# Hash attention with two expert layers: the weights' conversion at other steps, the shares one operation a step, a q fetch from GpSimd

## The chip, the cores and the metric

The kernel runs on one core of a Trainium2 chip. The metric is the device time of one execution in microseconds. Of a kernel the median of several runs is compared, and one execution beside them is profiled. The engines are TensorE (PE in the profile; its weight loads are PEld), VectorE (DVE), ScalarE (ACT), GpSimd (POOL) and SyncE (SP), which only issues DMAs. Each works through its own queue in order.

## The reference

Three layers in a row, all in float32:

```
bits(x)  = (x @ proj > 0)                        6 bits a token, for q and k
s        = q k^T / 8, masked to -1e9 where the buckets of q and k differ
attn     = softmax(s) @ v                        batch 2, 8 heads, 768 tokens, head size 64
x        = attn, heads joined                    1536 x 512
g        = elu(x @ w_in) @ w_out                 512 -> 2048 -> 512 (w_in, w_out drawn as float64)
p        = probs / (sum(probs) + 1e-9)           1536 x 4, the experts' shares
out      = sum_e p[:, e] * (relu(g @ w1[e]) @ w2[e])    4 experts, 512 -> 1024 -> 512
```

## The kernel before, in words

Every product is made of float32 values split in a high and a low part, three matmuls for one. The schedule is written out by hand: the program text gives the order of each engine's queue (`manual_schedule`), and semaphores between the queues are put in from the tiles that operations read and write. A tile is taken from a pool under a tag; a tag of a pool with one buffer (`bufs=1`, as pool `l1`) gives all its tiles the same place, one after the other.

**Attention** runs over 8 pairs of heads, 12 steps a pair (`PU`), 96 steps in all (`NU`); a step is 128 queries of one head. `att_step(u)` emits, in the order of `ORDER`: the combination of a finished half (C, `emit_comb`: ACT copies two parts out of PSUM, the second into `t1`, pool `l1`, and POOL adds them), the exponential of step u+1 (E), PE's transposes of step u (T, t), the scores of step u+2 (Q, into one PSUM bank), their minimum on DVE (N), the split of the transposed weights (H, h on ACT; L, l on DVE), a preparation (M, m, d) and a third of the product with v (V). The preparations of a pair stand at fixed steps i of the pair before it: step 0 transposes the sums of the last pair and sends them through DRAM (`prep_n`: DMA `d<-rt`, then two broadcasts `rx<-d` into the tile `rx`, tag "rx" of pool `l1`), steps 1 and 2 transpose q of the next pair (ACT copies it to `xt`, POOL splits it), step 3 makes the hash bits of q and k, steps 10 and 11 transpose k of the pair after.

`loads_step` then issues SP's DMAs: the loads of v, k and q (`load_v`, `load_qk`; i = 0, 1, 2, 4) and the placement of the next pair's q, k and bits (`place`, `place_bits`; i = 2, 3, 11). At i = 3 and 6 (`FIN_AT`) it emits `emit_fin`, which on POOL multiplies half of the last pair's result by `rx` and splits it; on i = 8 and 9 POOL splits v.

After it, in pairs 1 to 7, the list `pre` is worked off: the conversion of the first three tiles of `w_in` and `w_out` from 64-bit words to float32 (`conv_w`: 2 operations on ACT, 10 on DVE, 2 on POOL; then `consumed`, which issues the next load of raw weights on SP; then `split_w`, 4 on POOL), 18 entries for one tile. `PRE_AT` lists the steps of a pair at which one entry is taken (pairs 1 to 3 for the first tile, 4 to 6 for the second); `LASTN` gives the number of entries at each step of the last pair, for the third tile. In the last pair's second half TensorE also does the first matmuls with the first tile (`l1_start(0)`, behind step 6).

The experts' shares are made of `dp`, the domain probabilities, a tile of pool `l1` under the tag "rx" too, loaded at the start: six small DVE operations into `sm` and then `pn`, which is read at 483 us. They are emitted together after step 10 (`u == PU - 2`). The first tile `rx` is allotted at step 12.

`first()` is the start: pair 0 is loaded and prepared, then SP is given the load of v, of k of pair 1, the placements of pair 0's second head, v again and the load of q of pair 1 (`load_qk(1, "q")`, L624). The tiles `sk` and `sq` have one buffer each.

Of the kernel before, what the change touches and what calls it, by code (L numbers as in the profile page):

```python
# [13 lines left out]
ALU = mybir.AluOpType  # L14
PSUM = bass.MemoryType.PSUM

P = 128
# [18 lines left out]
def lsh_attention_moe_kernel(  # L36
# [14 lines left out]
    nc = tc.nc  # L51
    B, H, S, D = q.shape
# [3 lines left out]
    E = dprobs.shape[1]  # L56
    NJ = S // P
# [48 lines left out]
    def pair(g2):  # L106

        return g2 % B, g2 // B

    def load_qk(g2, nm):  # L110
        b, hp = pair(g2)
        t = st_p.tile([P, NJ, 2, D], F32, tag="s" + nm, name="s" + nm)
        x = {"k": k, "q": q}[nm][b, 2 * hp:2 * hp + 2]
        if g2:
            nc.sync.dma_start(out=t, in_=x.rearrange("h (p j) d -> p j h d", j=NJ))
        else:
            t = t.rearrange("p j h d -> p (j h d)").rearrange("p (h j d) -> p h j d", h=2, j=NJ)
            nc.sync.dma_start(out=t, in_=x.rearrange("h (p j) d -> p h j d", j=NJ))
        raws[g2, nm] = t

    def load_v(g2, par):
        b, hp = pair(g2)
        t = st_v.tile([P, NJ, D], F32, tag="sv", name="sv")
        nc.sync.dma_start(out=t, in_=v[b, 2 * hp + par].rearrange("(p j) d -> p j d", j=NJ))
        raws[g2, par] = t
# [19 lines left out]
    dp = l1.tile([P, B * NJ, E], F32, tag="rx", name="dp")  # L145
# [7 lines left out]
    def emit_proj():  # L153
        for i in range(2):
            r, c0 = slice(i * D, (i + 1) * D), 96 + i * HB
            c = slice(c0, c0 + NB)
            hi, lo = pj[0][r, c], pj[1][r, c]
            nc.vector.tensor_copy(hi, prj[r])
            nc.vector.tensor_tensor(out=lo, in0=prj[r], in1=hi.bitcast(F32), op=ALU.subtract)
            for t in pj:  # L160
                nc.vector.tensor_scalar(out=t[r, c0 + NB:c0 + HB], in0=t[r, c].bitcast(F32), scalar1=-1.0,
                                        scalar2=None, op0=ALU.mult)
# [9 lines left out]
        x_tiles(c)  # L172
    pn = const.tile([P, B * NJ, E], F32, name="pn")

    def emit_probs():
        sm = const.tile([P, B * NJ], F32, name="psum_e")
        nc.vector.tensor_add(sm, dp[:, :, 0], dp[:, :, 1])
        for e in range(2, E):
            nc.vector.tensor_add(sm, sm, dp[:, :, e])
        nc.vector.tensor_scalar(out=sm, in0=sm, scalar1=1e-9, scalar2=None, op0=ALU.add)  # L180
        nc.vector.reciprocal(out=sm, in_=sm)
        nc.vector.tensor_tensor(out=pn, in0=dp, in1=sm.unsqueeze(2).to_broadcast([P, B * NJ, E]),
                                op=ALU.mult)

# [111 lines left out]
    def mtile():  # L298
        return (ps_m if mc[0] % 2 or mc[0] >= LASTC else ps_v).tile([P, 512], F32, tag="a", name="m")
# [6 lines left out]
    def prep_t(g2, nm, ps, j0, n):  # L306

        src = raws[g2, nm]

        def pe():  # L310
            for i in range(n):
                x = src[:, j0 + i].rearrange("p h d -> p (h d)")
                nc.tensor.transpose(ps[:, i * P:(i + 1) * P], x, ident)

        if j0 == 0:
            for part in "hl":
                stg[nm + part] = ld.tile([P, S], F32R, tag=nm + part, name=nm + part)
        cs = slice(j0 * P, (j0 + n) * P)
        hi, lo, x = stg[nm + "h"][:, cs], stg[nm + "l"][:, cs], ps[:, 0:n * P]
        sc = 1.0 if nm == "k" else -scale  # L320
        if g2:
            def act():
                xt = st_v.tile([P, HS], F32, tag="xt", name="xt")
                nc.scalar.activation(out=xt, in_=x, func=ACTF.Copy, scale=sc)
                pool_split(hi, lo, xt)

            return pe, act, None
        return (pe, lambda: nc.scalar.activation(out=hi, in_=x, func=ACTF.Copy, scale=sc),
                lambda: nc.vector.scalar_tensor_tensor(out=lo, in0=x, scalar=sc, in1=hi.bitcast(F32),
                                                       op0=ALU.mult, op1=ALU.subtract))  # L330
# [14 lines left out]
    def bits_at(g2, nm, par, half):  # L345

        r = (2 * "kq".index(nm) + half) * 32 + par * HB
        t = (ks_t if nm == "k" else qs_t)[sl(g2, par)]
        return stg["b"][r:r + HB].bitcast(F32), t[D:KM, 1, half * HS:(half + 1) * HS]

    def place_bits(g2, nm, par):
        for half in range(2):
            src, dst = bits_at(g2, nm, par, half)
            nc.sync.dma_start(out=dst.bitcast(F32), in_=src)
# [146 lines left out]
    PU = 2 * NJ  # L501
# [6 lines left out]
    EX = 0  # L508
    EU = 0
    PRE_EVERY = 3  # L510
    LASTN = (1, 2, 2, 1, 2, 1, 2, 2, 2, 1, 1, 1)
    FIN_AT = (3, 6)
    PRE_AT = (3, 4, 5, 7, 8, 9)
    MSTEP = [None] * PU
    for i, st in zip(M_AT, (("n",), ("t", "q", 0), ("t", "q", UC), ("h",), ("t", "k", 0), ("t", "k", UC))):
        MSTEP[i] = st
# [45 lines left out]
    def first():  # L562

        z = a4.tile([P, 512], BF16, tag="mk2", name="z")
        nc.gpsimd.memset(z, 0.0)
        pz = ps_v.tile([P, 512], F32, tag="a", name="pz")

        def warm(n):
            for _ in range(n):
                mm(pz, z[:, 0:P], z, start=True, stop=True)  # L570

        warm(WARM[0])
        for t in pj:
            nc.vector.memset(t.bitcast(F32), 0.0)

        for n, nm in enumerate("kq"):
            t = a4.tile([P, NJ, 2, D], F32, tag=f"mk{n}", name="s0")
            x = raws[0, nm].rearrange("p h j d -> p j h d")
            for half in range(2):
                js = slice(half * UC, (half + 1) * UC)  # L580
                if half:
                    nc.vector.tensor_copy(t[:, js], x[:, js])
                elif nm == "k":
                    nc.scalar.copy(t[:, js], x[:, js])
                else:
                    nc.gpsimd.tensor_copy(t[:, js], x[:, js])
            raws[0, nm] = t
        emit_proj()
        los = []
        for nm, pool, tags in (("k", ps_t, ("pt0", "pt1")), ("q", ps_t, ("pt2", "pt3"))):  # L590
            for half in range(2):
                ps = pool.tile([P, 512], F32, tag=tags[half], name="p" + nm)
                pe, act, dve = prep_t(0, nm, ps, half * UC, UC)
                pe()
                act()
                los.append(dve)
            if nm == "k":
                for f in los:
                    f()
                for i in range(2):  # L600
                    nc.gpsimd.tensor_scalar(out=ks_t[0][0:D, i], in0=stg["kh"][0:D].bitcast(F32), scalar1=1.0,
                                            scalar2=1.0, op0=ALU.mult, op1=ALU.mult)
                nc.sync.dma_start(out=ks_t[0][D:P, 0].bitcast(F32), in_=stg["kl"][0:D].bitcast(F32))
        for f in los[2:]:
            f()
        nc.scalar.copy(qs_t[0][0:D, 0], stg["qh"][0:D].bitcast(F32))
        nc.scalar.copy(qs_t[0][D:P, 0], stg["qh"][0:D].bitcast(F32))
        nc.vector.tensor_copy(qs_t[0][0:D, 1], stg["ql"][0:D].bitcast(F32))
        load_v(0, 0)
        load_qk(1, "k")  # L610
        warm(WARM[1])
        pe, _, dve = prep_h(mtile())
        pe()
        dve()
        for (nm, half), f in zip((("q", 0), ("k", 0), ("k", 1), ("q", 1)),
                                 (nc.scalar.copy, nc.vector.tensor_copy, nc.vector.tensor_copy, nc.scalar.copy)):
            src, dst = bits_at(0, nm, 0, half)
            f(dst, src)
        warm(WARM[2])
        for nm in "kq":  # L620
            place(0, nm, 1)
            place_bits(0, nm, 1)
        load_v(0, 1)
        load_qk(1, "q")  # L624

    first()
    for par in range(2):
        split_v(0, par)
    nc.sync.dma_start(out=dp.rearrange("p (b j) e -> p b j e", b=B),
                      in_=dprobs.rearrange("(b p j) e -> p b j e", b=B, j=NJ))  # L630
# [9 lines left out]
    def att_step(u):  # L640
# [36 lines left out]
        if g2 >= 1 and m <= NPRE and u < NU:  # L677
            if i == 0 and k_ == 0:
                pre[:] = conv_w(0, m, cv_p, 2) + [lambda: consumed(0, m, False)]
                pre.extend(lambda n=n: split_w(0, m, wpool(m), "pP", n) for n in range(2))  # L680
                pre.append(lambda: consumed(0, m, True))
            for _ in range(i in PRE_AT if m < NPRE else LASTN[i]):
                if pre:
# [489 lines left out]
        if nm in "Vk":  # L1173
            at[nm] += 1

    fin, outq = [], []
    for u in range(NU - 2):
        att_step(u)
        if u == PU - 2:
            emit_probs()  # L1180
        if u == NU - PU - 1:
            early.close()
            for i in range(2):
                raw_free.append(open_pool(f"raw{i + 2}", 1, "right"))
            open_pool("wm", 1, "right")
            loads()
        if u == NU - PU + 6:
            l1_start(0)
        take(parts, 1)
# [52 lines left out]
```

## Time and profile before

| | us |
|---|---|
| median of 3 runs (range) | 1047.69 (1045.72 to 1051.52) |
| profiled execution | 1047.5 |
| its span, first to last instruction | 1045.7 |
| PE busy | 1016.3 (97%) |
| DVE busy | 831.8 (80%) |
| ACT busy | 521.1 (50%) |
| POOL busy | 513.1 (49%) |

Attention takes the first 250 us or so, the first dense layer the time to 515, the experts the rest. Busy shares of the whole span are means over these parts. The granted clock of TensorE was 0.994 of full speed in the mean.

### The profile page before, as it was taken

How to read it: one execution, taken by the hardware profiler on the slowest of the kernel's cores; microseconds unless marked ns; L12 is line 12 of the kernel's file. 1: busy time of each engine (PE TensorE's matmuls, PEld its weight loads, DVE VectorE, ACT ScalarE, POOL GpSimd, SP SyncE). 2: the span in 40 equal slices, each digit the busy share in tenths (PEclk: the TensorE clock that was granted, in tenths of full speed). 3: DMA queues.
4: the chain of work that ended last, by engine and by line, in shares of the span. 5: the costliest groups of instructions: out<-in, count | busy, mean ns of one | idle time of the engine just before them, and what ended most of it. 6: DMA issues, size and time to landing. Idle time of an engine off the chain costs nothing.

```text
span 1045.7 us, 16064 instructions
## 1 busy us (share of the span) xinstructions
PE 1016.3 (97%) x5886; PEld 889.8 (85%) x5886; DVE 831.8 (80%) x1289; ACT 521.1 (50%) x1024; POOL 513.1 (49%) x428
## 2 busy tenths in 40 slices
PE   7999999999998999999999999999999999999996
PEld 5898999888876888888889999898898889988896
DVE  6889889988586888734557779888898888989885
ACT  5898899898564445434532333332423233233322
POOL 3466776666354345432321245545555546364554
PEclk9999999999998999999999999999999999999999
DMA  6857576561031222200020030020201102020012
GB/s 177 163 135 158 131 171 147 128 192 48 1 111 51 81 81 81 81 1 22 9 83 1 1 102 11 8 74 11 91 11 41 42 11 92 11 74 8 1 51 71
DMA packets 72694, 72.24 MB, mean 69 GB/s; under 512 B 26132, under 2 KB 60648, under 8 KB 72616
## 3 DMA queue, kind: packets, MB, share of 16 engines
q1 hardware_dynamic: 72312, 71.14, 24.7%
q8 instruction: 47, 0.77, 0.3%
q14 instruction: 31, 0.25, 0.1%
q10 hardware_dynamic: 304, 0.07, 0.0%
HBM read 48.98 MB, written 3.21 MB: 50 GB/s over the span
## 4 chain that ended last, share of the span: by engine, by line
PE 32%; issue 10%; POOL 7%; DVE 7%; ACT 1%; POOLq 0%
PE l L1018 15%; POOL a L1034 4%; PE a L967 3%; PE a L966 3%; PE a L965 3%; PE r L967 2%; PE r L966 2%; PE r L965 2%; DVE w L907 2%; DVE temps L994 1%; POOL h L750 1%; POOL hf L1000 1%; PE l L766 1%; POOL w L907 1%; DVE temps L996 1%
## 5 line engine op out<-in xcount | busy, mean ns | idle before, releaser
L1018 PEld LDWEIGHTS l<-w,op 128*128 128x128 f32 x2016 | 252.1, 188 | 13.3 <-ACT op L903 5.2
L1018 PE MATMUL l<-w,op 128*128 128x256 f32 x2016 | 255.5, 281 | 3.8 <-ACT op L903 3.8
L1034 POOL TENSOR_TENSOR a<-a,temps 128x512 f32<-128x512 f32 x84 | 124.3, 1502 | 60.0 <-DVE a L1029 60.0
L766 PE MATMUL l<-h,w 128*128 128x512 f32 x576 | 139.8, 391 | 0.1
L750 POOL TENSOR_TENSOR h<-g,h 128x512 fp32r<-128x512 f32 x44 | 66.7, 1516 | 143.2 <-ACT h L746 93.9
L766 PEld LDWEIGHTS l<-h,w 128*128 128x128 f32 x576 | 107.9, 188 | 24.5 <-POOL h L750 0.9
L1000 POOL TENSOR_TENSOR hf<-hf,temps 128x512 f32<-128x512 f32 x24 | 40.1, 1670 | 155.7 <-DVE op L907 146.9
L393 DVE TENSOR_SCALAR_CACHE_REDUCE mk<-s 128x768 f32<-128x768 f32 x96 | 91.3, 951 | 23.0 <-PE s L384 20.3
L903 ACT ACTIVATE op<-temps 128x512 fp32r<-128x512 f32 x48 | 30.1, 627 | 155.0 <-DVE temps L996 155.0
L426 DVE TENSOR_TENSOR ptl<-pt,pth 128x384 fp32r<-128x384 f32 x192 | 97.6, 550 | 11.0 <-ACT pth L429 11.0
L907 DVE TENSOR_TENSOR op<-hf,op 128x512 fp32r<-128x512 f32 x120 | 100.0, 849 | 4.4 <-ACT op L903 4.3
L903 ACT ACTIVATE op<-hf 128x512 fp32r<-128x512 f32 x120 | 74.1, 624 | 57.3 <-PE l L1018 29.9
L402 ACT ACTIVATE mk<-mk,mn 128x768 f32<-128x768 f32 x96 | 89.7, 935 | 11.5 <-DVE mk L393 10.9
L412 PE MATMUL pt<-cst,mk 128*128 128x128 f32 x576 | 94.9, 274 | 0.6 <-ACT mk L402 0.4
L383 PE MATMUL s<-ks,qs 128*128 128x512 f32 x192 | 80.2, 440 | 8.4 <-DVE mk L393 7.9
L429 ACT ACTIVATE pth<-pt 128x384 fp32r<-128x384 f32 x192 | 84.0, 482 | 8.3 <-PE pt L412 7.9
L412 PEld LDWEIGHTS pt<-cst,mk 128*128 128x128 f32 x576 | 71.0, 140 | 12.7 <-ACT mk L402 5.4
L967 PE MATMUL r<-xh,w 128*128 128x512 f32 x192 | 75.8, 395 | 0.0
L967 PE MATMUL a<-xh,w 128*128 128x512 f32 x192 | 75.6, 394 | 0.0
L966 PE MATMUL r<-xl,w 128*128 128x512 f32 x192 | 75.5, 393 | 0.0
L966 PE MATMUL a<-xl,w 128*128 128x512 f32 x192 | 75.4, 393 | 0.0
L965 PE MATMUL a<-xh,w 128*128 128x512 f32 x192 | 75.1, 391 | 0.0
(154 smaller groups left out, 2228.0 us busy)
## 6 DMA issues: line engine op xcount, KB each, us to landing
raw<-in_moe_w_dram SPq DMA_DIRECT2D x32, 512.0 KB
raw<-in_moe_w_in_dram SPq DMA_DIRECT2D x16, 512.0 KB
raw<-in_moe_w_out_dram SPq DMA_DIRECT2D x16, 512.0 KB
ks<-kh SPq DMA_DIRECT2D x15, 384.0 KB
qs<-qh SPq DMA_DIRECT2D x30, 192.0 KB
sk<-in_k_dram SPq DMA_DIRECT2D x8, 384.0 KB
sq<-in_q_dram SPq DMA_DIRECT2D x8, 384.0 KB
ks<-kl SPq DMA_DIRECT2D x16, 192.0 KB
```

The costliest lines, as they stand in the source:

```text
L393: nc.vector.tensor_scalar(out=e_t[u], in0=s_t.pop(u)[:, 0:S], scalar1=MASKED, scalar2=None, op0=ALU.min, op1=ALU.min, accum_out=mn)
L402: nc.scalar.activation(out=e, in_=e, func=ACTF.Exp, bias=mn_t.pop(u), scale=-1.0, accum_out=sums_t[g2][:, j, par:par + 1])
L412: nc.tensor.transpose(pt[:, i * P:(i + 1) * P], e_t[u][:, kb * P:(kb + 1) * P], ident)
L426: nc.vector.tensor_tensor(out=lo, in0=pt, in1=hi.bitcast(F32), op=ALU.subtract)
L766: mm(ps, a, b_, start=(m == 0 and n == 0), stop=(m == GS[g] - 1 and n == 2))
L903: nc.scalar.activation(out=hi, in_=x, func=ACTF.Copy)
L907: e.tensor_tensor(out=lo, in0=x, in1=hi.bitcast(F32), op=ALU.subtract)
L965: mm(ps, wh[:, cs], xh[c][:, ts], start=(c == 0), stop=False)
L966: mm(ps, wh[:, cs], xl[c][:, ts], start=False, stop=False)
L967: mm(ps, wl[:, cs], xh[c][:, ts], start=False, stop=(c == NC - 1))
L1018: mm(ps[:, tt * HD:(tt + 1) * HD], a[:, cs], b_[:, k_], start=(n == 0), stop=(n == 11))
L1034: nc.gpsimd.tensor_tensor(out=x, in0=x, in1=keep[nm], op=ALU.add)
```

## The change

q of pair 1 is fetched by a DMA that GpSimd issues, ahead of pair 0's hash bits, in place of the last of SP's DMAs in `first()`. The six operations of the shares are emitted one a step, behind steps 14 to 19 (from `u >= PU + 2` on). `PRE_AT` and `LASTN` are other lists, with the same sums.

```diff
-    def load_qk(g2, nm):
+    def load_qk(g2, nm, eng=nc.sync):
...
         if g2:
-            nc.sync.dma_start(out=t, in_=x.rearrange("h (p j) d -> p j h d", j=NJ))
+            eng.dma_start(out=t, in_=x.rearrange("h (p j) d -> p j h d", j=NJ))
...
-    def emit_probs():
+    def probs_steps():
         sm = const.tile([P, B * NJ], F32, name="psum_e")
-        nc.vector.tensor_add(sm, dp[:, :, 0], dp[:, :, 1])
+        yield nc.vector.tensor_add(sm, dp[:, :, 0], dp[:, :, 1])
         for e in range(2, E):
-            nc.vector.tensor_add(sm, sm, dp[:, :, e])
...
+            yield nc.vector.tensor_add(sm, sm, dp[:, :, e])
+        yield nc.vector.tensor_scalar(out=sm, in0=sm, scalar1=1e-9, scalar2=None, op0=ALU.add)
+        yield nc.vector.reciprocal(out=sm, in_=sm)
+        yield nc.vector.tensor_tensor(out=pn, in0=dp, in1=sm.unsqueeze(2).to_broadcast([P, B * NJ, E]), op=ALU.mult)
...
-    LASTN = (1, 2, 2, 1, 2, 1, 2, 2, 2, 1, 1, 1)
+    LASTN = (2, 1, 2, 0, 1, 1, 2, 2, 2, 2, 2, 1)
     FIN_AT = (3, 6)
-    PRE_AT = (3, 4, 5, 7, 8, 9)
+    PRE_AT = (3, 4, 6, 7, 9, 10)
...
         load_v(0, 0)
         load_qk(1, "k")
+        load_qk(1, "q", nc.gpsimd)
         warm(WARM[1])
...
         load_v(0, 1)
-        load_qk(1, "q")
...
-    fin, outq = [], []
+    fin, outq, probs = [], [], probs_steps()
     for u in range(NU - 2):
         att_step(u)
-        if u == PU - 2:
-            emit_probs()
+        if u >= PU + 2:
+            next(probs, None)
```

## Rows read from the trace of the kernel before

**Rows 1.** Busy time by stretch: PE, PEld, DVE, ACT, POOL, clock, DMA, GB/s

```profile
47.00:250.00 203.00, 196.34 (x1282) 178.42 (x1283) 179.03 (x375) 181.56 (x412) 131.91 (x152) 1.00 0.60 141
...
312.00:330.00 18.00, 12.98 (x46) 9.93 (x47) 12.09 (x18) 7.73 (x14) 6.91 (x4) 0.81 0.30 99
```

**Rows 2.** Timeline of PE, 0 to 60: start, us, what, [idle before <-releaser]

```profile
25.07 0.55 PE L313 MATMUL m<-cst,sq 128*128 128x128 f32 x3 [2.29 <-DMA sq<-in_q_dram]
...
47.91 0.50 PE L383 MATMUL s<-ks,qs 128*128 128x512 f32 x1 [1.20 <-DVE mk L393]
...
49.53 0.27 PE L469 MATMUL m<-cst,sums 128*12 128x128 f32 x1 [0.33 <-DVE sums L462]
```

**Rows 3.** Waits from 50 to 250: total us, times, longest

```profile
PE s L383 <- DVE mk L393: 4.6, 6, 0.9
```

**Rows 4.** Timeline of PE in the last pair

```profile
239.37 0.50 PE L383 MATMUL s<-ks,qs 128*128 128x512 f32 x1 [0.73 <-DVE mk L393]
242.37 0.50 PE L383 MATMUL s<-ks,qs 128*128 128x512 f32 x1 [0.67 <-DVE mk L393]
```

**Rows 5.** Timeline of SP's queue at the start

```profile
19.24 0.70 SPq L115 DMA_DIRECT2D sq<-in_q_dram  x1
```

**Rows 6.** Timeline of POOL at the start

```profile
7.30 1.63 POOL L601 TENSOR_SCALAR ks<-kh 64x768 fp32r<-64x768 f32 x2 [1.11 <-ACT kh L328]
11.81 0.51 POOL L135 TENSOR_SCALAR vs<-sv 128x384 fp32r<-128x384 f32 x1 [2.88 <-DMA sv<-in_v_dram]
...
21.23 0.51 POOL L135 TENSOR_SCALAR vs<-sv 128x384 fp32r<-128x384 f32 x1 [7.83 <-DMA sv<-in_v_dram]
...
29.32 1.01 POOL L136 TENSOR_TENSOR ql<-xt,qh 128x384 fp32r<-128x384 f32 x1
```

**Rows 7.** Timeline of DVE behind step 10

```profile
44.60 0.29 DVE L177 TENSOR_TENSOR psum_e<-dp 128x12 f32<-128x12 f32 x1
...
46.52 0.46 DVE L182 TENSOR_TENSOR pn<-dp,psum_e 128x48 f32<-128x48 f32 x1
46.90 0.94 DVE L393 TENSOR_SCALAR_CACHE_REDUCE mk<-s 128x768 f32<-128x768 f32 x1
```

**Rows 8.** Timeline of DVE at the end of step 19

```profile
68.88 0.42 DVE L247 TENSOR_SCALAR w<-w 128x512 f32<-128x512 f32 x1
```

**Rows 9.** Timeline of SP's queue, pairs 1, 2 and 4

```profile
52.15 1.29 SPq L477 DMA_DIRECT2D rx<-d  x2
...
83.19 1.27 SPq L477 DMA_DIRECT2D rx<-d  x2
...
90.71 1.47 SPq L354 DMA_DIRECT2D qs<-hb  x2
...
99.44 0.69 SPq L115 DMA_DIRECT2D sq<-in_q_dram  x1
...
144.24 1.27 SPq L477 DMA_DIRECT2D rx<-d  x2
```

**Rows 10.** Timeline of POOL, pairs 1 and 4

```profile
58.07 1.02 POOL L487 TENSOR_TENSOR u<-u,rx 128x384 f32<-128x384 f32 x1
...
64.74 1.01 POOL L457 TENSOR_TENSOR u<-u,t 64x384 f32<-64x384 f32 x1 [3.97 <-ACT t L456]
...
148.74 1.01 POOL L487 TENSOR_TENSOR u<-u,rx 128x384 f32<-128x384 f32 x1 [1.29 <-DMA rx<-d]
```

**Rows 11.** Timeline of ACT at step 21

```profile
70.63 0.49 ACT L456 ACTIVATE t<-pv 64x384 f32<-64x384 f32 x1
```

**Rows 12.** Timeline of PE at steps 22 and 25

```profile
72.09 0.55 PE L412 MATMUL pt<-cst,mk 128*128 128x128 f32 x3
...
80.99 0.49 PE L313 MATMUL m<-cst,sq 128*128 128x128 f32 x3
```

**Rows 13.** Busy time by stretch, columns as in rows 1

```profile
319.00:323.00 4.00, 0.73 (x2) 0.30 (x2) 4.00 (x6) 1.21 (x2) 2.76 (x2) 0.69 0.35 102
323.00:327.40 4.40, 4.37 (x10) 3.47 (x11) 0.58 (x1) 0.00 (x0) 0.00 (x0) 0.51 0.37 146
```

More of the change, by code (lines that the diff above doesn't have):

```diff
@@ L173, in lsh_attention_moe_kernel @@
     pn = const.tile([P, B * NJ, E], F32, name="pn")
-    def emit_probs():
+    def probs_steps():
         sm = const.tile([P, B * NJ], F32, name="psum_e")
-        nc.vector.tensor_add(sm, dp[:, :, 0], dp[:, :, 1])
+        yield nc.vector.tensor_add(sm, dp[:, :, 0], dp[:, :, 1])
         for e in range(2, E):
-            nc.vector.tensor_add(sm, sm, dp[:, :, e])
[L180 to L183, printed above, removed]
+            yield nc.vector.tensor_add(sm, sm, dp[:, :, e])
+        yield nc.vector.tensor_scalar(out=sm, in0=sm, scalar1=1e-9, scalar2=None, op0=ALU.add)
+        yield nc.vector.reciprocal(out=sm, in_=sm)
+        yield nc.vector.tensor_tensor(out=pn, in0=dp, in1=sm.unsqueeze(2).to_broadcast([P, B * NJ, E]), op=ALU.mult)
     wide = w_in.dtype != F32
```

## The prediction

> **What bounds the kernel now.** I read the stretches first, then TensorE's waits in the attention part, then the four queues around the steps that the change touches. TensorE (PE) works 196.3 of the 203 us from 47 to 250; the next stretch with much idle time is 312 to 330 (13.0 of 18) [rows 1], where it waits for weights that VectorE and ScalarE convert in their own queues behind attention, so that this moves along. Whatever makes PE stand still in attention is thus added to the end, and an idle stretch that goes is gained. The pauses that the change can reach are few. One of 2.29 us is for the q of the second pair at 25.07, with 1.20 and 0.33 us at steps 11 and 12, where VectorE (DVE) is late [rows 2]. Between 50 and 250 PE waits six times for DVE before a scores matmul, 4.6 us in all [rows 3], of which 0.73 and 0.67 fall in the last pair [rows 4]; the other 3.2 us are four waits in pairs 2 and 5. Times below are of the profiled execution, whose own 1047.5 us is 0.2 under the median of 1047.69.
>
> **The q fetch on GpSimd.** On SP the fetch is issued at 19.24, behind the placements of pair 0, and PE has to wait for it until 25.07 [rows 2, 5]. On GpSimd (POOL) it stands behind two copies that end at about 9 [rows 6], so the data can be there 10 us sooner, and PE would reach that point at 22.8. What its issue occupies POOL with, no row shows: on SP it takes 0.70 us [rows 5]; from above, POOL stands idle 2.88 and 7.83 us in front of the two v splits [rows 6], so some 10 us cost nothing. The bytes are the same and only come earlier among transfers with slack. Behind it POOL's chain cannot move as far as PE: the second v split still waits for its own transfer until 21.23; five splits from there on (v, two of k, two of q, 0.51 + 1.01 us and a gap, 1.55 each) end at 29.0, where they ended at 30.33 [rows 6]. So the gain lies between 1.3 and 2.3 us if POOL is free in time; I take 2.0, since only the last quarter of the hash matmuls, PE's next use, needs the last split.
>
> **The shares, taken out of step 10.** Six operations stand in DVE's queue from 44.60 to 46.98, 2.4 us, ahead of the minimum that frees the scores' bank [rows 7]. PE pays 1.20 and 0.33 us for it [rows 2]. That goes: -1.5 us (bounds 0 and -1.5).
>
> **The shares, put at steps 14 to 19: the part that costs.** The input of the shares, `dp`, lies in the one buffer that carries the tag "rx". The next tile of that tag, `rx`, is allotted at step 12, and its first writers are two broadcast DMAs on SP. In the kernel before, the shares are done at step 10, so the buffer is free. Now its last reader, the product into `pn`, stands at step 19. I take it that a tile's buffer is handed on only after all readers of the old tile, wherever they stand in the text; then SP stops at the first of these DMAs from step 12 to step 19, with everything behind it.
> When does it go on? DVE's step 19 ends with the conversion at 68.88 + 0.42 = 69.3 [rows 8]. To that come the product's 0.46 [rows 7] and what of the other five operations (1.9 us) DVE's idle time doesn't take: it idles 203 - 179 = 24 us over some 84 steps [rows 1], 0.29 a step, 1.4 in five; 0.5 stays. So the DMAs go at about 70.4 in place of 52.15 [rows 9].
> Who waits, in order: (a) POOL. The normalisation at step 15 (58.07) reads `rx`. From the issue of the two to POOL's go it takes 4.5 us (144.24 to 148.74) [rows 9, 10], so it starts at 74.9. Behind it stand its split (0.51 + 1.0 us) and the add of step 18, which ran at 64.74: 1.0 + 1.6 + 1.0, with gaps 3.7, to 78.6. (b) ScalarE (ACT). The copy at 70.63 writes `t1`, of which there is one, and that add reads it [rows 11]. So ACT stands from 70.63 to 78.6, 8.0 us, and the exponential behind it is late for PE's transposes of step 22 (72.09) [rows 12]. (c) SP itself. The sequence from the broadcast to the next pair's bits takes 90.71 + 1.47 - 83.19 = 9.0 us where SP issues it back to back, a pair later [rows 9], so the bits leave SP at 79.4 and land within the 3.2 us that the broadcast needs after its last issue (4.5 less 1.3); PE wants them in the scores right behind those transposes, from 80.1 on. That is about the same time, no second stall of size. (d) The end of SP's sequence, the q of pair 3, is issued 99.44 - 83.19 = 16.25 us after the broadcast [rows 9], at 86.65, and with the same 4.5 us it is there at 91.15. PE wants it at 80.99 [rows 12]: 10.2 us of delay in all, (a) to (c) being inside it. Should it take as long as pair 1's q (19.24 to 25.07 [rows 2, 5]) it is 11.5; with a faster landing, 8.0 remain. After a wait of about 8 us PE's clock will be low: after the two waits before 323 it was granted 0.51, the 1.2 GHz level, for 4.4 us [rows 13]. That costs at most 2.2 us, and lies inside the wait of (d), as 80.99 + 8.0 + 2.2 is 91.2. I take 10.2, bounds 7.5 and 13. Nothing gives it back, as PE is full afterwards [rows 1].
>
> **The conversion's new steps.** In the last pair the steps ahead of the first weights' matmuls get fewer operations on DVE (two at step 4 become one), against waits of 0.73 and 0.67 [rows 4]: -1.2, bounds -1.8 and +1. The GpSimd splits of that tile come at most one step later, still in attention, where their first reader stands behind it, and the raw load that the conversion sets free is issued one step later: nothing, as two other raw tiles are converted first. In pairs 1 to 6 three of six steps move by one; POOL works in the new ones as well, so of the 3.2 us in four waits I take 0.5, bounds -3.2 and +1.5.
>
> **Sum.** 1047.5 - 2.0 - 1.5 - 1.2 - 0.5 + 10.2 = 1052.5 us, 0.5% over the median.
>
> **Rivals.** *The broadcast doesn't wait* (the buffer is handed on in the order of the text). For it: six steps with one small operation each are harmless in every row; against it: the one buffer, and that `pn` would then be made from overwritten data. It gives the savings alone less the 0.5 that DVE can't hide: 1047.5 - 5.2 + 0.5 = 1042.8, not slower than before; with the waits of pairs 2 and 5 gone, 1040. *POOL held by its own fetch*, the slower side: POOL writes 1536 pieces of 256 bytes (128 partitions x 6 x 2). It needs about 9.4 us for its six splits (two v, two k, two q) before PE's use at some 29, so from 19.6 on, that is from 10.6 us of occupation on, each us more costs one; at 16 us that is 5.4, the saving of 2.0 and 3.4 more: 1052.5 + 5.4 = 1057.9. For it: no row bounds its issue; against: a queue that has nothing but the fetch to do for 10 us. *The wait is there but short*: SP is let go at step 19 and only the first stall stays, since q lands faster; 8.0 in place of 10.2, and one us more of the four waits gone: 1047.5 - 5.2 - 1.0 + 8.0 = 1049.3.
>
> On the fetch, the trace has no DMA from GpSimd, and the nearest rows are the idle stretches of POOL [rows 6]. The Trainium skill (SBUF — State Buffer, section on its two separate sides) says that a DMA from the GpSimd queue has its descriptors written by GpSimd, and that VectorE operations in a two-port mode lock it out meanwhile; its example goes from 620 to 3100 ns. By that, as an estimate, the fetch would land 2.5 us later, at about 16, still ahead of 22.8, and the sum stays; with many such locks it feeds the second rival. No run here shows it.
>
> **Chances.** A measurement of this kernel tells 0.5%, 5.2 us, from no change. The forecast 0.66: around 1052.5 with 3 us to each side, so about half of it is under 1052.9 (same 0.33) and half over (slower 0.33). No wait 0.21 (faster 0.14, same 0.07). POOL held 0.06 (slower). Short wait 0.07 (same). That makes faster 0.14, same 0.47, slower 0.39. The forecast's own range is 1048 to 1057; to leave out no more than two in ten the range goes down into the first rival and up to the second: 1042 to 1058.
>
> **What would show it.** Right: SP idle some 17 us in front of the first broadcast, released by DVE's product; POOL's first normalisation near 71 on the new clock (74.9 less the 3.5 saved before it); one PE pause of 7 to 8 us at step 22, a stretch of low clock, a second one of 1 to 3 us for q of pair 3; no pause at 22.8 and none at 47.9. Wrong: broadcasts issued at step 12 as before, and no PE pause over 1 us between 45 and 95. Then the time is 1043 or below. If PE waits for q or for POOL's splits between 20 and 30, the fetch is mis-sized.

## The result and the profile after

The changed kernel takes 1055.12 us (median of 7 runs, 1053.76 to 1060.19), the kernel before 1047.07 beside it (7 runs, 1044.59 to 1051.52): ratio 1.009, 95% interval 1.0072 to 1.0108. The forecast was 1052.5 in 1042 to 1058. By the 0.5% that the prediction names as its own measure this is slower, to which it gave 0.39, against 0.47 for no change. The profiled execution took 1057.06 us, 1.9 above the median, and its span is 1055.3, so that differences between the two traces come out larger than between the medians (9.6 against 8.05 us). The line numbers of the changed kernel are one less than before from the shares on.

SP's queue, with the row that answers to [rows 9] (start, us, what):

```profile
49.09 0.77 SPq L473 DMA_DIRECT2D d<-rt  x1
67.75 1.29 SPq L476 DMA_DIRECT2D rx<-d  x2
...
76.05 1.47 SPq L353 DMA_DIRECT2D qs<-hb  x2
...
85.21 0.70 SPq L115 DMA_DIRECT2D sq<-in_q_dram  x1
```

The first broadcast went at 52.15 before; now SP stands still from 49.9 to 67.75, with the loads and placements of the next pair queued behind it. What lets it go is on DVE, the last operation of the shares [rows 7]:

```profile
67.53 0.20 DVE L182 TENSOR_TENSOR pn<-dp,psum_e 128x48 f32<-128x48 f32 x1
```

The broadcast starts 0.02 us after that. The stop then travels through GpSimd (POOL) and ScalarE (ACT) [rows 10, 11]:

```profile
71.88 0.99 POOL L486 TENSOR_TENSOR u<-u,rx 128x384 f32<-128x384 f32 x1 [15.95 <-DMA rx<-d]
...
74.50 0.98 POOL L456 TENSOR_TENSOR u<-u,t 64x384 f32<-64x384 f32 x1
```

```profile
75.52 0.49 ACT L455 ACTIVATE t<-pv 64x384 f32<-64x384 f32 x1 [6.59 <-POOL u L456]
```

It reaches TensorE (PE) as two pauses. The last two of these rows answer to [rows 12]; the first three stand at the start, in the first, second and third scores:

```profile
12.61 0.47 PE L382 MATMUL s<-ks,qs 76*128 76x512 f32 x1 [0.97 <-ACT qs L618]
...
14.26 0.50 PE L382 MATMUL s<-ks,qs 128*128 128x512 f32 x1 [1.06 <-DVE mk L392]
...
16.38 0.66 PE L382 MATMUL s<-ks,qs 128*128 128x512 f32 x1 [0.51 <-DVE mk L392]
...
76.98 0.90 PE L411 MATMUL pt<-cst,mk 128*128 128x128 f32 x3 [6.32 <-ACT mk L401]
...
89.79 0.52 PE L312 MATMUL m<-cst,sq 128*128 128x128 f32 x3 [2.05 <-DMA sq<-in_q_dram]
```

The waits of 1.06 and 0.51 are in the trace of before too, 1.1 us earlier; the one of 0.97 is new. The row of before:

```profile
13.20 0.50 PE L383 MATMUL s<-ks,qs 128*128 128x512 f32 x1 [1.06 <-DVE mk L393]
```

The stretches, columns as in [rows 1] (the third from the end is PE's granted clock, 0.50 being its 1.2 GHz level):

```profile
18.00:20.00 2.00, 2.00 (x10) 1.94 (x9) 1.95 (x4) 1.28 (x3) 0.00 (x0) 0.51 1.02 257
...
47.00:250.00 203.00, 189.81 (x1232) 172.70 (x1230) 167.98 (x358) 175.96 (x398) 124.55 (x146) 0.98 0.59 141
...
77.00:81.00 4.00, 4.00 (x16) 3.81 (x17) 3.21 (x7) 3.13 (x8) 3.83 (x6) 0.50 0.47 97
...
321.00:339.00 18.00, 12.93 (x44) 9.81 (x44) 11.98 (x18) 7.62 (x14) 6.92 (x4) 0.81 0.26 95
```

From 47 to 250 PE works 6.5 us less than before, and it runs at half clock after the pause at 77, and also once at the start, where the trace of before has 1.00 from 9 to 30 us. The stretch that stood at 312 to 330 [rows 1] comes 9 us later with the same idle time (12.93 busy against 12.98), so nothing is paid back there: the span ends 9.6 us later.

Where the time went is best seen step by step: the start of the scores matmul that `att_step(u)` emits, after minus before, in the two traces. "First" is the first scores matmul of all, "second" the one behind it.

| place | after minus before, us | what happened |
|---|---|---|
| first, second scores | -0.1, +1.1 | DVE's copy at the start late |
| u = 3 | +2.2 | PE at the low clock |
| u = 4 | -0.3 | the wait for q is gone |
| u = 13 | -2.1 | shares out of step 10: -1.8 |
| u = 21 | -1.6 | shares and new steps of the conversion on DVE: +0.5 |
| u = 23, u = 26 | +6.6, +8.8 | the two pauses: +10.4 |
| pairs 2, 4, 5 | -0.75, +1.3, -0.75 | new steps of the conversion |
| last pair, end of the span | +9.1, +9.6 | last pair alone +0.4 |

The block from the buffer's wait is what was forecast (10.4 against 10.2), and so are the shares (-1.8 against -1.5). The other three terms, -3.7 in the forecast, came to nothing in these two traces: -0.3 for the fetch, -0.2 and +0.4 for the two lists. Why is the question of most experiments.

### The profile page after: what moved, and what is told of

It is laid out like the page before. It is cut to its first block, busy times and chain, and to the rows that moved or that the text cites. A ratio compares the mean times of both kernels' runs of the same rounds, so it can differ in the third digit from the quotient of the medians.

```text
span 1055.3 us, 16064 instructions
## 1 busy us (share of the span) xinstructions
PE 1020.3 (97%) x5886; PEld 893.5 (85%) x5886; DVE 832.2 (79%) x1289; ACT 521.9 (49%) x1024; POOL 511.2 (48%) x429
## 4 chain that ended last, share of the span: by engine, by line
PE 31%; issue 10%; POOL 7%; DVE 7%; ACT 1%; POOLq 0%
PE l L1017 14%; POOL a L1033 4%; PE a L966 3%; PE a L965 3%; PE a L964 3%; PE r L966 2%; PE r L965 2%; PE r L964 2%; DVE w L906 2%; DVE temps L993 1%; POOL h L749 1%; POOL hf L999 1%; PE l L765 1%; POOL w L906 1%; DVE temps L995 1%
```

## Experiments

Twelve kernels in three groups, each compared with its own runs of the kernel before: own_dp, late_product, shares_from11 and shares_step10 with a median of 1047.43 (23 runs); q_gpsimd, q_act, pre_at and lastn with 1046.91 (35); q_sp_early and the three kernels with parts together with 1046.82 (35).

### The shares and the buffer

**own_dp**: the changed kernel, with `dp` loaded into the tile of `pn` and multiplied in place, so that no buffer is shared with `rx`.

```diff
-    dp = l1.tile([P, B * NJ, E], F32, tag="rx", name="dp")
+    dp = pn = const.tile([P, B * NJ, E], F32, name="pn")
```

> The changed kernel, with the shares' input loaded into the tile of the result, pn, and multiplied there in place, so that it no longer lies in the one buffer of rx; nothing else differs. Theory (SP waits at the first broadcast for the buffer's last reader): broadcasts issued at about 50 in place of 67.75, POOL's 15.95 us and ACT's 6.59 us of idle time gone, PE's pauses of 6.32 and 2.05 us gone, the time down by about 10.4 to 1044.7 (1043 to 1046.5). Rival (the six operations between the steps, or the order of the queues, cost the time): unchanged at 1055.

Measured: 1049.12 us (12 runs, 1043.84 to 1052.53), ratio 1.0003 [0.9985, 1.002]. SP's queue in its trace:

```profile
53.47 1.29 SPq L475 DMA_DIRECT2D rx<-d  x2
```

The broadcast goes at step 12 again, and from 47 to 95 us PE has no pause over 0.42 us. So the buffer is the cause of the stop. The time missed the expected 1043 to 1046.5: five runs lie between 1043.8 and 1046.3, at a mean granted clock of 0.993 to 0.996, and seven between 1048.9 and 1052.5, at 0.989 to 0.991; the trace is of the first kind. The rest of the change, freed of the stop, is thus not faster than the kernel before.

**late_product**: the kernel before, and only the product into `pn` moved, to step 19. The other five operations stay at step 10, the fetch and both lists are as before.

```diff
-        nc.vector.tensor_tensor(out=pn, in0=dp, in1=sm.unsqueeze(2).to_broadcast([P, B * NJ, E]),
-                                op=ALU.mult)
...
+        if u == PU + 7:
+            emit_pn()
```

> The kernel before, with only the last of the six operations, the product into pn, put behind step 19; the other five stay behind step 10. Theory: this one late reader of the buffer is enough: SP stops for some 17 us, PE pauses about 6 to 7 us at step 22 and 2 us for q of pair 3, +10 us: 1057. Rival (the wait comes from something else in the change): 1047.

Measured: 1056.93 us (4 runs, 1055.73 to 1058.67), ratio 1.0095 [1.0082, 1.0108]. One operation of 0.20 us costs 9.5 us in the median. DVE, SP and PE in its trace:

```profile
68.59 0.20 DVE L185 TENSOR_TENSOR pn<-dp,psum_e 128x48 f32<-128x48 f32 x1
```

```profile
68.81 1.29 SPq L480 DMA_DIRECT2D rx<-d  x2
```

```profile
78.06 0.90 PE L415 MATMUL pt<-cst,mk 128*128 128x128 f32 x3 [6.32 <-DMA qs<-qh]
...
90.94 0.52 PE L316 MATMUL m<-cst,sq 128*128 128x128 f32 x3 [1.64 <-DMA sq<-in_q_dram]
```

It is the same pair of pauses without any other part of the change; by steps it goes from -0.5 (u = 21) to +10.0 (u = 26), 10.5 us.

**shares_from11**: the changed kernel, with the shares begun at step 11, so that the product stands at step 16.

```diff
-        if u >= PU + 2:
+        if u >= PU - 1:
```

> The changed kernel with the six operations behind steps 11 to 16 in place of 14 to 19. Theory: the broadcasts go at about 61, POOL's add is ready just when ACT wants t1 (no pause at step 22), but q of pair 3 is issued 17.5 us after the broadcasts and lands 4.6 us later, at 83, where PE wants it at 79: 3 to 4 us of the 10.4 stay, 1048.5. Rival (only POOL and ACT pass the wait on, SP's own queue has slack): 1044.7. Rival (the price is fixed, whatever the length of the wait): 1055.

Measured: 1052.26 us (6 runs, 1047.81 to 1053.81), ratio 1.0044 [1.0029, 1.006]. Its SP issues the broadcast at 62.25, about 5.5 us earlier than in the changed kernel; the pause at step 22 is gone (0.39), and the one for q of pair 3 stays:

```profile
72.60 0.55 PE L411 MATMUL pt<-cst,mk 128*128 128x128 f32 x3 [0.39 <-ACT mk L401]
...
84.87 0.87 PE L312 MATMUL m<-cst,sq 128*128 128x128 f32 x3 [3.37 <-DMA sq<-in_q_dram]
```

By steps it costs 4.8 us (+0.4 to +5.2), the wait of 3.37 and a stretch at low clock behind it; the theory said 3 to 4, and the time is above its 1048.5. So the end of the wait is q's arrival, part (d) of the forecast, and the stall at step 22 lies inside it.

**shares_step10**: the changed kernel with the shares in one block behind step 10, as before.

```diff
-        if u >= PU + 2:
-            next(probs, None)
+        if u == PU - 2:
+            for _ in probs:
+                pass
```

> The changed kernel with the shares back in one block behind step 10; the fetch of q by GpSimd and the conversion's new steps stay. Theory: the 10.4 us of the wait go and PE's 1.5 to 1.8 us at steps 11 and 12 come back: 1046.3, so the other two parts together are worth less than 1 us. Rival (the fetch and the conversion's steps cost as well): 1048 or more. The sum as forecast for these two parts (3.7 us gained): 1043.4.

Measured: 1049.06 us (12 runs, 1046.64 to 1052.89), ratio 1.0024 [1.001, 1.0038]. No stop of SP (the broadcast goes at 51.35), and PE pays 1.22 and 0.33 at steps 11 and 12 as before. What is left of the change, the fetch and the two lists, is thus 0.24% slower than the kernel before, as the first rival said.

### The fetch of q

**q_gpsimd** and **q_act**: the kernel before, with the early fetch alone, issued by GpSimd or by ScalarE.

```diff
         load_qk(1, "k")
+        load_qk(1, "q", nc.gpsimd)        # q_act: nc.scalar
```

> The kernel before, with only the fetch of q of pair 1 issued by GpSimd. The changed kernel's trace shows PE 1.06 us later at its second scores, where a DVE copy took 1.74 us in place of 0.55 while GpSimd issued the fetch, then a stretch of low clock (1.2 us more), and the 2.5 us of waiting for q gone. Theory (the issue on GpSimd blocks that copy and the start loses what the fetch gains): 0.3 us faster to 2 us slower than before, 1047 to 1049, with the copy at about 1.7 us. Rival (the fetch keeps its 2.0 us as forecast, and the changed kernel's slow start has another cause): 1045.4.

> The kernel before, with the same fetch at the same place, but issued by ACT. Theory (GpSimd's issue blocks DVE's copy): the copy takes 0.55 us again, the second scores are on time, the wait for q is gone: 2 us faster, 1045.4. Rival (the bytes that come earlier delay the placements and the k of pair 1, whoever issues them): 1047 or more, with the second scores or the k transposes late.

Measured: q_gpsimd 1051.95 (12 runs, 1045.21 to 1052.85), ratio 1.0033 [1.0017, 1.0049]; q_act 1048.24 (11 runs, 1044.42 to 1050.38), ratio 1.0016 [1.0005, 1.0026]. The first scores in the two traces, q_gpsimd and then q_act:

```profile
15.98 0.76 PE L383 MATMUL s<-ks,qs 128*128 128x512 f32 x1 [3.97 <-DMA ks<-kl]
```

```profile
13.00 0.47 PE L383 MATMUL s<-ks,qs 128*128 128x512 f32 x1 [1.12 <-DMA ks<-kl]
```

Before, they start at 11.16 without a wait. The transfer `ks<-kl`, which SP issues 1.2 and 1.7 us after the fetch in these traces (9.34 after 8.18, 9.21 after 7.56), lands late in both, whoever issues the fetch; in late_product, with no fetch ahead of it, it is issued at 9.32, and PE goes at 12.12 without a wait. So the bytes do not "only come earlier among transfers with slack". In the trace of the changed kernel SP had issued it at 8.24, the fetch went at 8.74, and PE doesn't wait for it; nor does it in own_dp and shares_from11, where SP issues it 0.4 us behind the start of the fetch: no order holds between the two queues. But there is another cost, which only the GpSimd variant can have. DVE of the kernel before, then DVE and POOL of the changed kernel:

```profile
9.29 0.55 DVE L608 CAST qs<-ql 64x768 fp32r<-64x768 f32 x1
```

```profile
9.18 1.74 DVE L607 CAST qs<-ql 64x768 fp32r<-64x768 f32 x1
```

```profile
8.74 1.80 POOL L115 DMA_DIRECT2D sq<-in_q_dram  x1
```

The copy takes 0.55 us in the trace of q_gpsimd, where it begins behind the issue (at 10.27, the issue being 8.18 to 9.98). Here it begins inside the issue, 1.36 us before its end, and ends 0.38 after it. In the other three traces where it begins inside the issue it ends 0.38 after it too: it takes 1.62 in shares_step10, 0.82 in own_dp and 0.89 in shares_from11. In q_act it takes 0.55, as the theory said, but the time is the rival's. My expectation for q_gpsimd missed, the copy of 1.7 in its trace and the 1047 to 1049 in its median. Of q_gpsimd's 12 runs, eight took 1051.8 to 1052.9 at a mean granted clock of 0.988 to 0.990, and four 1045.2 to 1047.3 at 0.993 to 0.996. The trace is one of the eight; that the four differ from it in the start is likely, but no trace shows it.

**q_sp_early**: the kernel before, with the fetch left on SP and moved up behind the load of k of pair 1, so behind `ks<-kl`.

```diff
         load_qk(1, "k")
+        load_qk(1, "q")
...
         load_v(0, 1)
-        load_qk(1, "q")
```

> The kernel before with one edit: the fetch of q of pair 1 stays on SP but is issued right behind the load of k of pair 1, some 9 us earlier, and so behind the transfer of ks<-kl that TensorE needs for its first scores (issued at 8.35 in the trace of before). Theory A (the gain of the early fetch was eaten by its bytes standing ahead of that urgent transfer, and on GpSimd by the copy that its issue blocks): issued behind it, the fetch delays nothing that is urgent, TensorE's 2.29 us wait for q at step 4 goes, the first scores and the step after stand within about 1 us of before (two traces without any edit of the start differ from before by 1.0 to 1.1 there), and all steps behind step 4 come about 2 us earlier: some 1045.5 us, ratio 0.998. Rival B (the wait is not for q alone: a fetch in the start costs what it saves, wherever it stands, since later placements and v come later by its issue): the wait for q goes, but another of 1 us or more takes its place before step 6, and the time is 1047 to 1048.5.

Measured: 1047.66 (12 runs, 1046.29 to 1052.07), ratio 1.0013 [0.9998, 1.0028]. The wait for q is gone, nothing waits for `ks<-kl`, and still the time is B's. Neither theory gives the reason: no other wait of 1 us or more has taken the place of the one for q. Stretches of its trace, columns as in [rows 1]:

```profile
16.00:18.00 2.00, 1.84 (x7) 1.39 (x6) 0.37 (x2) 1.40 (x3) 0.00 (x0) 0.50 1.04 197
18.00:20.00 2.00, 2.00 (x11) 2.00 (x10) 1.77 (x4) 1.11 (x3) 0.00 (x0) 0.50 0.83 194
20.00:22.00 2.00, 2.00 (x9) 1.81 (x9) 0.91 (x2) 1.22 (x4) 0.00 (x0) 0.50 1.00 201
```

PE is granted its 1.2 GHz level for these 6 us and falls from 1.1 us late at the start to 3.0 at u = 3; at u = 4, the wait for q gone, +0.5. All eight traces with the early fetch show such a stretch between 15 and 25 us, and one of the six without it (pre_at below: 3.0 late at u = 3, no wait for q, +0.5 at u = 4, the very same). In the other four without it (late_product, lastn, two_parts, three_parts) the wait for q is 0.66 to 0.81, not the 2.29 of the trace of before. Fetch and use in lastn, whose first scores stand within 0.15 us of before's:

```profile
18.94 0.70 SPq L115 DMA_DIRECT2D sq<-in_q_dram  x1
```

```profile
23.31 0.55 PE L313 MATMUL m<-cst,sq 128*128 128x128 f32 x3 [0.66 <-DMA sq<-in_q_dram]
```

From the issue to PE's go it takes 4.37 us here, 4.38 to 4.43 in the other three, and 5.83 in the trace of before (19.24 to 25.07 [rows 2, 5]). The three others have their first scores 1 us later than before, with no edit near the start, and their fetch is issued 0.9 to 1.05 later too. The row of three_parts:

```profile
24.61 0.55 PE L312 MATMUL m<-cst,sq 128*128 128x128 f32 x3 [0.80 <-DMA sq<-in_q_dram]
```

So 1.4 of the 2.29 us are a slow landing in the one execution that was profiled before, and stand in every difference to its trace. What an early fetch can take away is 0.7 to 0.8 us as a rule, and the stretch at low clock costs more: with the same late start q_sp_early stands 1.0 us behind late_product and three_parts at u = 4.

### The two lists

**pre_at** and **lastn**: the kernel before with the one list or the other.

```diff
-    PRE_AT = (3, 4, 5, 7, 8, 9)
+    PRE_AT = (3, 4, 6, 7, 9, 10)
```

```diff
-    LASTN = (1, 2, 2, 1, 2, 1, 2, 2, 2, 1, 1, 1)
+    LASTN = (2, 1, 2, 0, 1, 1, 2, 2, 2, 2, 2, 1)
```

> The kernel before, with only PRE_AT changed. From the step-by-step comparison of the changed kernel: 0.75 us won in pair 2 and again in pair 5, 1.3 us lost in pair 4, together 0.2 us faster: 1047.2, not to be told from no change. The forecast said 0.5 us faster.

> The kernel before, with only LASTN changed. From the step-by-step comparison of the changed kernel: 0.4 us slower over the last pair, 1047.8; with the fetch and shares also there but the wait gone it was 1.0 us faster over the same steps, 1046.4. The forecast said 1.2 us faster, 1046.2.

Measured: pre_at 1049.01 (11 runs, 1046.56 to 1049.63), ratio 1.0015 [1.0006, 1.0023], a little slower; lastn 1046.34 (11 runs, 1044.09 to 1047.21), ratio 0.9993 [0.9984, 1.0001], by its time not to be told from no change, its last pair 1.0 us shorter in the trace. By steps, pre_at costs 1.2 in pair 1 and 1.25 in pair 4 and gains 0.75 in pairs 2 and 5. The reason is on DVE. Two of its conversions in pair 1 of pre_at, and POOL at the same time:

```profile
69.80 0.98 DVE L247 TENSOR_SCALAR w<-w 128x512 f32<-128x512 f32 x1
...
76.70 1.25 DVE L248 TENSOR_SCALAR w<-w 128x512 int32<-128x512 int32 x1
```

```profile
69.49 1.01 POOL L136 TENSOR_TENSOR vs<-sv,vs 128x384 fp32r<-128x384 f32 x1
...
76.66 1.00 POOL L136 TENSOR_TENSOR kl<-xt,kh 128x384 fp32r<-128x384 f32 x1
```

The operation takes 0.42 elsewhere [rows 8]. Here it ends 0.28 (70.78 to 70.50) and 0.29 us (77.95 to 77.66) after the GpSimd operation within which it began. This holds throughout: of the 18 such operations (`w<-w` and `raw<-w`) between 50 and 250 in the trace of before, eleven begin within a GpSimd operation. Two of these begin in its last 0.03 us and keep their 0.42; the other nine take 0.62 to 1.32, and each ends 0.28 to 0.36 us after it. Where the conversion is first it is GpSimd that is held: in own_dp both begin at 75.33, the conversion takes 0.42 and the GpSimd operation 1.28, where it takes 1.01 alone. One of the nine stands ahead of a wait that I had left unexplained in pair 2 [rows 3]; DVE, POOL and PE of the kernel before:

```profile
94.03 1.32 DVE L252 TENSOR_SCALAR raw<-w 128x512 int32<-128x512 int32 x1
```

```profile
93.99 1.00 POOL L457 TENSOR_TENSOR u<-u,t 64x384 f32<-64x384 f32 x1 [3.61 <-ACT t L456]
```

```profile
96.27 0.50 PE L383 MATMUL s<-ks,qs 128*128 128x512 f32 x1 [0.71 <-DVE mk L393]
```

In pre_at, where that conversion takes 0.53, this wait is gone. The other three waits of pairs 2 and 5 (103.93, 185.67 and 193.35) stand behind conversions too that begin 0.04 to 0.05 us behind a GpSimd operation and take 1.30 to 1.52; one of the three is the same operation, the other two have two inputs and take 0.68 elsewhere. So a list of steps is good or bad by where each conversion meets GpSimd. In pair 1 of pre_at the four conversions sum to 3.20 us against 1.90 before, 1.3 more for PE's 1.2. The Trainium skill (SBUF — State Buffer, section "Who interferes with whom") says that VectorE and GpSimd share one pair of ports, that between a GpSimd operation and a VectorE one in a two-port mode whichever starts first holds it for the whole instruction, and that the other is blocked fully; `cast` and `tensor_scalar` are among the operations it names as able to enter such a mode. These traces agree (0.42 becomes 1.25).

### Parts that should be good, together

All three are the kernel before with: **two_parts** the shares one a step with `dp` in the tile of `pn` (the edit of own_dp), and the new last list; **three_parts** also the new steps of the conversion, in pairs 2 and 5 only; **four_parts** also the fetch of q_sp_early.

```diff
-            for _ in range(i in PRE_AT if m < NPRE else LASTN[i]):
+            for _ in range(i in ((3, 4, 6, 7, 9, 10) if k_ == 1 else PRE_AT) if m < NPRE else LASTN[i]):
```

> The kernel before with the shares one operation a step from step 14 on, dp loaded into the tile of pn and multiplied in place (so that no buffer is shared with rx), and the new list for the last pair; the list of the other pairs and the fetch of q are as before. Theory A (the parts are independent, and the stop of SP alone ate their gain): -1.8 from step 10 and -1.0 in the last pair, both read from traces of other variants, so 2.8 us: some 1044.2 us, ratio 0.9973, and no stop of TensorE over 1 us between steps 11 and 30. Rival B (the end absorbs a part: what TensorE gains in attention is taken back where the weights' conversion bounds it, at 312 to 330): the steps of attention are 2.8 us earlier, the end only 1 to 1.5, some 1046 us.

> As the kernel with two parts, and of the new steps of the conversion only those of pairs 2 and 5, where the trace of the variant with the new list alone showed -0.75 and -0.75; pairs 1, 3, 4 and 6 keep the old list (in pairs 1 and 4 the new one cost 1.2 and 1.25). Theory A (each pair's steps act for themselves): 1.5 us under the kernel with two parts, some 1042.7 us, ratio 0.9959. Rival B (the gains in pairs 2 and 5 are only a part of the losses of pairs 1 and 4 given back): nothing beside the kernel with two parts, within 0.5 us.

> As the kernel with three parts, with the fetch of q on SP right behind the load of k. Theory A (all four add up): 2 us more, some 1040.7 us, ratio 0.994. Rival B (the early fetch costs what it saves): within 0.5 us of the kernel with three parts, some 1042.7.

Measured: two_parts 1045.85 (12 runs, 1044.22 to 1046.63), ratio 0.9987 [0.9975, 0.9998]; three_parts 1044.38 (12 runs, 1043.84 to 1045.63), ratio 0.9974 [0.9962, 0.9987], the fastest of all; four_parts 1046.07 (12 runs, 1043.78 to 1048.85), ratio 0.9986 [0.9971, 1.0001]. Three parts give the 1.5 over two that A said (1.3 by steps from pair 2 on), so pairs act for themselves. With the fetch as a fourth the median is 1.7 higher, outside both A and B: the fetch gives nothing here either. Its trace has PE at 0.50 from 16 to 22 and stands 1.1 us behind three_parts at u = 4. It loses another 1.4 in the last pair, where its conversions meet GpSimd operations (0.98 for 0.42 at 239.21) and those of three_parts don't (0.42 at 238.24).

Two parts give 1.0, not 2.8. The end did not absorb it (B): the last pair is 2.1 us early and the span 2.0 shorter, the slow landing in the trace of before included. What is missing was lost at steps 19 to 22. PE, DVE and POOL of two_parts:

```profile
64.48 0.50 PE L382 MATMUL s<-ks,qs 128*128 128x512 f32 x1 [0.57 <-DVE mk L392]
...
71.89 0.50 PE L382 MATMUL s<-ks,qs 128*128 128x512 f32 x1 [0.52 <-DVE mk L392]
```

```profile
62.50 1.05 DVE L179 TENSOR_SCALAR psum_e<-psum_e 128x12 f32<-128x12 f32 x1
...
69.83 1.13 DVE L247 TENSOR_SCALAR w<-w 128x512 int32<-128x512 int32 x1
```

```profile
62.46 1.00 POOL L456 TENSOR_TENSOR u<-u,t 64x384 f32<-64x384 f32 x1 [3.25 <-ACT t L455]
...
69.67 1.00 POOL L456 TENSOR_TENSOR u<-u,t 64x384 f32<-64x384 f32 x1 [1.98 <-ACT t L455]
```

An operation on 12 elements takes 1.05 us, since it begins 0.04 after a GpSimd operation does; in the changed kernel, where POOL stands idle at that time, the same takes 0.16. Out of step 10 the shares give 1.8; between steps 18 and 23 1.45 of it is given back. In own_dp, with the new steps of the conversion as well, 0.7 is given back from step 18 to step 25, less than the 1.45 of two_parts and less than the 1.2 of the new steps alone in pre_at: such prices don't add.

## Why the prediction was right, point by point

**Right: the shares put at steps 14 to 19.** "SP stops at the first of these DMAs from step 12 to step 19" held to 0.02 us, and late_product shows that the last reader alone does it. The chain (a), (b) and (d) came in order: the normalisation at 71.88 (forecast near 71), PE's pause of 6.32 (forecast 7 to 8, so shorter), the low clock behind it, a second pause of 2.05 (1 to 3). It ends with q of pair 3, as shares_from11 shows, and the sum was 10.4 against 10.2. That the two are so near is in part luck, as two errors cancel. Without the stop PE would have wanted q at 79.4 (80.99 less the 1.6 won by then); the broadcast went 11.7 us ahead of that, where the forecast has 10.6, and from it to the issue of q it took 17.46 us, where the forecast has 16.25. One link differs: the last release before PE's first pause is the exponential in the changed kernel and `qs<-qh` in late_product, two ends of one stop.

**Right: the shares taken out of step 10**, -1.8 against -1.5. **Half right: that DVE hides them but for 0.5.** The changed kernel loses 0.5 at these steps, with POOL stopped, but conversions of the new list stand beside the shares there (64.97, 67.19), and the two are not told apart. With POOL running it was 1.45 in two_parts.

**Wrong: the q fetch, "the bytes are the same and only come earlier among transfers with slack", -2.0.** It was -0.3 in the changed kernel's trace, and alone, in three forms, it is 0.13 to 0.33% slower in the ratio (for SP's form the interval reaches below 1). Two things failed. The wait of 2.29 was read from one execution, in which the transfer took 5.83 us from issue to use; in four others it took 4.37 to 4.43, and the wait was 0.66 to 0.81. And the early fetch has a price that the sum put at nothing: a stretch at 1.2 GHz follows it in all eight traces (why is open), and `ks<-kl` is late in two. On GpSimd its issue also held DVE's copy until 0.38 us after its end, the reverse of the lock that the prediction cited, where VectorE would hold GpSimd up.

**Wrong: the conversion's new steps, -0.5.** Alone they are +0.95 by steps and 1.0015 in the ratio, inside the stated bounds (-3.2 and +1.5). I priced a moved operation by its row of 0.42 and did not look at what GpSimd does beside it; the rows that show it stood in the trace (94.03, 1.32 us). In the changed kernel pair 1's part falls into the stop and can't be told from it.

**Mis-sized: the last list, -1.2.** By steps it is -0.9 to -1.0 in five traces (lastn, own_dp, shares_step10, two_parts, three_parts) and +0.4 in three (the changed kernel, shares_from11, four_parts). In the changed kernel's there are three waits of 0.91, 0.43 and 0.41 in place of the two in [rows 4], and conversions of 1.24 at 243.95 and 1.08 at 248.93 beside GpSimd operations. So the same list gains or loses by what it meets.

The savings of -3.7 for fetch and lists were thus about nothing; that is why the time lies above 1052.5, by 2.6, and still within the 3 us that the forecast allowed around it. Of the rivals, "the broadcast doesn't wait" fell with the row at 67.75. "POOL held by its own fetch" fell in its form: the issue takes 1.80, not more than 10.6. "Short wait" fell with the second pause; only the first stall was to stay in it.

Open: why the granted clock falls at the start of every trace with the early fetch, and of pre_at without it. In q_sp_early and in three_parts PE's matmuls and waits are alike up to 15 us, a wait of 1.06 included, and only the first of them falls to 0.50.

## What to carry to other kernels

When an operation is moved later, look up which tile it reads, and who is given that tile's buffer next: a reader of 0.2 us at the wrong place stopped a DMA queue for 18 us, and cost some 10. A wait for a transfer that one execution shows may be a slow landing of that execution (2.29 us here, 0.66 to 0.81 in four others); before it is counted as a gain, look at it in a second one, and ask what comes next when it is gone. On DVE the price of a copy or of an operation with a scalar depends on the GpSimd operation that runs beside it, up to 0.9 us on 0.42 here, and 1.2 on a copy's 0.55; a schedule by hand has to place the two apart.

## What the runs showed of the hardware

- A DVE `TENSOR_SCALAR` of the conversion (128x512, tile to tile in SBUF) that begins within a GpSimd operation ends 0.28 to 0.36 us after it (nine of 18 in the trace of before), so that 0.42 became 1.25; one on 12 elements ended 0.09 after it, so that 0.16 became 1.05. The four waits of pairs 2 and 5 in [rows 3] that I could not place stand behind conversions held in this way. One that reads PSUM (`hb<-m`) takes 0.68 beside a GpSimd operation (56.55 in two_parts) as without one (56.73 in the changed kernel).
- GpSimd's issue of a DMA in 1536 pieces took 1.80 us (SP 0.70 [rows 5], ScalarE 0.68 in q_act). In all four traces where a DVE copy of 0.55 began within it, the copy ended 0.38 us after it, at most 1.74 long.
- With an early transfer of 393 KB issued 1.7 or 1.2 us ahead of it, a small transfer came late for PE, by 1.12 and 3.97 us; issued 0.5 us ahead of the large one or 0.4 behind the start of its issue (the changed kernel, own_dp, shares_from11) it was not waited for.
- The same transfer at the same place took 4.37 to 4.43 us from issue to use in four executions and 5.83 in another.
